# Attention times v on 64x32 array tiles instead of 64x64, in a talking-heads and Fourier-mix kernel

## The chip, the cores and the metric

One core of a Trainium2 chip. The metric is the device time of one execution in microseconds (us). The kernel before takes 2300.06 us, the median of three runs (2299.63 to 2300.28).

The engines are TensorE (PE, with its weight loader PEld), VectorE (DVE), ScalarE (ACT), GpSimd (POOL) and SyncE (SP, which only issues DMAs). PE multiplies a stationary operand, loaded by LDWEIGHTS, with a moving operand that streams through. Its array of 128 rows and 128 columns can be cut into tiles that work side by side: a "64x32" matmul uses 64 rows (the contraction) and 32 columns (the output partitions), so eight of them fill the array; of "64x64" ones four do. The names in the profile, such as `64*64`, are rows times columns of the matmul.

## The reference, cut to what matters

All data is float32. Eight batches, 12 heads, 448 positions, head dimension 64.

```python
scores = scale * np.matmul(q, k.transpose(0, 1, 3, 2))
scores = np.einsum('bhij,hg->bgij', scores, w_pre)       # heads mixed
attn = softmax(scores)
attn = np.einsum('bhij,hg->bgij', attn, w_post)          # heads mixed again
x = np.matmul(attn, v)                                   # the changed product
# then, with x as (8, 448, 768):
mixed = real(fft over channels of fft over positions of x)
u = x + mixed
un = layer_norm(u)
out = u + relu(un @ w_ch1) @ w_ch2                       # 768 -> 3072 -> 768
```

## The kernel before, in words

The program has two phases. The first does the attention and the Fourier mix (`mix_phase`), up to some 800 us; the second (`ffn_phase`) does the normalisation and the two large products, and isn't touched by the change. The weights are split and combined on DVE and POOL beside both phases.

**Steps.** The first phase runs 184 steps, 23 for each batch. A step handles some rows of the scores for all 12 heads. Its parts on PE are: the premix (`emit_premix`, L656; tile `mx`), the postmix of an earlier step (`emit_postmix`, L690; tile `po`), and the scores of a later block (`emit_qk`, L628; PSUM tiles `ms`). These three are issued as matmuls of 64 or 60 rows by 32 columns. DVE takes the maximum of `mx` (L663), ACT the exponential into `PP` (L670), DVE the reciprocal of the sums (L678), POOL the scaling (L680), and after the postmix DVE transposes `po` in blocks of 32 into the tile `Pv` (L703).

**Attention times v.** Once six or so steps have filled `Pv` (a group of two blocks), `emit_av` is called three times, each for two heads in each half of the head range (a pair `pr`): 8 batches x 4 groups x 3 pairs = 96 visits. A visit has seven key blocks (`jb`), which accumulate in PSUM. The two halves of the partitions (`y`) hold different heads and write to two PSUM tiles, `pss[0]` and `pss[1]`; the two heads of a half (`x`) write to output partitions 0 to 63 and 64 to 127. So it is 7 x 2 x 2 = 28 matmuls of 64 rows by 64 columns. The moving operand is a strided view of `Pv`: runs of five floats, 24 or 20 of them 224 floats apart, which makes 120 or 100 columns. The stationary operand is a 64x64 block of `v`. ACT then copies both PSUM tiles into `XT` (L489, the helper that all such copies share).

In the trace each of these float32 matmuls shows as two passes, each with its own weight load: 56 passes for a visit, 16 for a premix, a postmix or a score part.

**Other users of PE in this phase.** Transposes (L601, L764) and the two Fourier stages (L829, L845) have tile shapes of their own, with up to 128 rows and columns.

**Order.** On PE, DVE, ACT and POOL the order of the instructions is that of the program (a manual schedule). Two lists (`ORDERS`) say what each even and odd step does in which order; tables of steps (`AT_AV`, `AT_QK` and so on) say in which step each visit, score part, transpose and Fourier stage falls. The PSUM tiles `ms` come from a pool of four; every visit takes two.

Of the kernel before, what the change touches and what calls it, by code (L numbers as in the profile page):

```python
# [16 lines left out]
P = 128  # L17
B, NH, S, D = 8, 12, 448, 64
# [11 lines left out]
R = 5  # L30
# [119 lines left out]
def _ap(t: bass.AP, offset: int, dims) -> bass.AP:  # L150
    return bass.AP(tensor=t.tensor, offset=t.offset + offset,
                   ap=[list(d) for d in dims])
# [6 lines left out]
def _row(t: bass.AP) -> int:  # L159
    return t.ap[0][0]  # L160
# [290 lines left out]
def mix_phase(ctx, tc, rest, ident, q, k, v, w_pre, w_post, u_scr, u_rev, wts, lead):  # L451
# [36 lines left out]
    def copy(eng, out, in_):  # L488
        (nc.scalar.copy if eng == "a" else nc.vector.tensor_copy)(out=out, in_=in_)  # L489
# [11 lines left out]
    def ms_tile():  # L501
        return ms[-1]()
# [205 lines left out]
    def emit_av(a, pr):  # L708

        b, k = divmod(a, NG)  # L710
        st = batches[b]
        Pv = turned[a]["Pv"]
        rp = _row(Pv)
        nu = (GROUP_AT[k + 1] - GROUP_AT[k]) * 4
        pss = [ms_tile() for _ in range(2)]
        for jb in range(C7):
            for x in range(2):
                for y in range(2):
                    i = 2 * pr + x
                    nc.tensor.matmul(  # L720
                        pss[y][64 * x:64 * x + 64, :nu * R],
                        st["v", pr][64 * y:64 * y + 64, x, jb * D:(jb + 1) * D],
                        _ap(Pv, 64 * y * rp + 32 * jb + R * i,
                            [[rp, 64], [HS, nu], [1, R]]),
                        start=(jb == 0), stop=(jb == C7 - 1))
        g = groups[b * NG + BLOCKS[2 * k][3]]
        if pr == 0:
            g["XT"] = pxt.tile([P, 6, XW], F32, name="XT", tag="XT")
        XT = g["XT"]
        rx = _row(XT)  # L730

        def done(y):
            rs = _row(pss[y])
            c = 0
            for _, w, n, _, first, sg in BLOCKS[2 * k:2 * k + 2]:
                dst = _ap(XT, (3 * y + pr) * XW + PG[g["gi"]] + first,
                          [[rx, P], [sg * w, R], [sg, w]])
                src = _ap(pss[y], c, [[rs, P], [1, R], [R, w]])
                copy(ENG["AV"][y], dst, src)
                c += R * w  # L740
            if y == 1 and pr == 2:
                if k in SPILL:
                    gi, c0, n, go, co = SPILL[k]
                    Xo = groups[b * NG + go]["XT"]
                    back = -1 if gi == 2 else 1
                    nc.scalar.copy(
                        out=_ap(Xo, PG[go] + co, [[rx, P], [XW, 6], [1 - 2 * (go == 1), n]]),
                        in_=_ap(XT, PG[gi] + c0, [[rx, P], [XW, 6], [back, n]]))
                if k in NONE:
                    gi, cols = NONE[k]  # L750
                    for o in cols:
                        Xo = groups[b * NG + gi]["XT"]
                        nc.vector.memset(Xo[:, :, PG[gi] + o:PG[gi] + o + 1], 0.0)
        return [lambda y=y: done(y) for y in range(2)]
# [136 lines left out]
    for b in range(B):  # L891
# [31 lines left out]
        for n in range(NG):  # L923
            for pr in range(3):
                due("AV", f + GROUP_AT[n + 1] + AT_AV[n][pr],
                    lambda a=b * NG + n, pr=pr: (emit_av(a, pr), None))
            at, gi = AT_X[n]
            if b == B - 1 and n > 1:
                at += 2
            due("full", f + at, lambda g=groups[b * NG + gi]: emit_x(g))  # L930
# [623 lines left out]
```

## Time and profile before

| | |
|---|---|
| Median of three runs | 2300.06 us |
| Span of the profiled execution | 2297.6 us, 60793 instructions |
| The profiled execution's own time | the page gives its span alone; the median is 2.5 us above it |
| Granted TensorE clock | 0.998 |
| PE, PEld busy | 2249.2 us (98%), 1740.7 us (76%) |
| DVE, ACT, POOL busy | 1711.2 us (74%), 1167.1 us (51%), 1292.1 us (56%) |
| L720 on PE | 160.8 us busy, 5376 passes, 62.9 to 797.0 us |

How to read it: a row of a timeline is start, duration, engine, line, operation, output <- input, tile (rows*columns), shape, and count; in brackets stands the engine's idle time before it and what ended it ("issue": nothing that the profile shows). A row of a group is count | busy us, mean ns of one | idle time before, by what ended it. A row of waits is who waited for whom: us in total, times, the longest. In a row of the windows the numbers after the window are its length and then the busy time and count of each engine named in the head of the view. The ends of matmuls are modelled, their starts are recorded. Busy times of a line on PE count time in which several of its passes run as one.

### The profile page before, as it was taken

What the parts mean: (1) busy time and instruction counts of PE and PEld (TensorE: products, weight loads), DVE (VectorE), ACT (ScalarE), POOL (GpSimd) and SP (SyncE); (2) the same over time, 40 slices, a digit from 0 to 9 for tenths busy, and PEclk for the clock granted to TensorE, in tenths of its full rate; (3) what the DMA queues carried; (4) which work ended last, traced back from release to release, by engine and by line L of the source; (5) the groups of instructions that cost most, each with busy time, mean ns of one, the idle gap of its engine ahead of it and who ended that gap; (6) DMA issues with size and microseconds to landing.
All of it is one profiled execution on the core that took longest, in us unless ns stands there. A gap on an engine that the chain in (4) does not pass through costs nothing.

```text
span 2297.6 us, 60793 instructions
## 1 busy us (share of the span) xinstructions
PE 2249.2 (98%) x22894; PEld 1740.7 (76%) x22894; DVE 1711.2 (74%) x3640; ACT 1167.1 (51%) x3330; POOL 1292.1 (56%) x1805
## 2 busy tenths in 40 slices
PE   7999999999999999999999999999999999999998
PEld 3455555555554677777899999999999899999998
DVE  5778787888877757776877787778778777765545
ACT  4676767767676533231445445444444445434434
POOL 7677878879768541221555555546555645454334
PEclk9999999999999999999999999999999999999999
DMA  7566565666756475649677887788787987795664
GB/s 185 168 178 181 168 192 171 190 179 181 202 151 190 143 265 182 230 162 327 191 181 180 252 214 184 212 195 242 204 197 184 277 188 174 191 257 121 143 146 76
DMA packets 228063, 439.45 MB, mean 191 GB/s; under 512 B 35964, under 2 KB 149558, under 8 KB 227772
## 3 DMA queue, kind: packets, MB, share of 16 engines
q1 hardware_dynamic: 156620, 301.52, 38.2%
q0 software_dynamic: 68864, 133.00, 30.4%
q8 instruction: 183, 3.00, 0.6%
q10 hardware_dynamic: 2288, 1.05, 0.2%
q14 instruction: 108, 0.88, 0.1%
HBM read 213.16 MB, written 143.16 MB: 155 GB/s over the span
## 4 chain that ended last, share of the span: by engine, by line
PE 87%; DVE 5%; DMA 3%; ACT 2%; issue 1%; POOL 1%; SPq 1%; ACTq 0%; DVEq 0%; POOLq 0%
PE psP L1213 18%; PE psP L1335 14%; PE psR L1213 9%; PE psR L1335 7%; PE mx L656 6%; PE ms L720 6%; PE ms L628 5%; PE po L690 5%; PE psQ L1213 4%; PE psQ L1335 3%; PE psP L1290 3%; PE ms L845 2%; PE ms L601 2%; DMA Kr<-Sb 1%; PE psR L1290 1%
## 5 line engine op out<-in xcount | busy, mean ns | idle before, releaser
L1369 POOL DMA_DIRECT2D out_dram<-od x172 | 209.1, 1276 | 261.7 <-DVE od L1357 175.3
L680 POOL TENSOR_SCALAR PP<-PP,rcp 128x448 f32<-128x448 f32 x368 | 234.6, 647 | 170.2 <-DVE rcp L678 123.8
L670 ACT ACTIVATE PP<-mx,nmx 128x448 f32<-128x448 f32 x368 | 230.2, 631 | 165.2 <-DVE nmx L663 157.2
L663 DVE TENSOR_REDUCE nmx<-mx 128x1 f32<-128x448 f32 x368 | 212.5, 618 | 101.2 <-PE mx L656 99.1
L1176 POOL TENSOR_TENSOR hq<-h 128x128 f32<-128x128 f32 (+1 forms) x210 | 130.0, 619 | 255.9 <-ACT h L1235 122.3
L1363 ACT COPY od<-psP 128x192 f32<-128x192 f32 x488 | 156.1, 320 | 172.0 <-PE psP L1335 170.6
L1366 DVE TENSOR_TENSOR od<-od 128x768 f32<-128x768 f32 x210 | 201.3, 972 | 52.7 <-ACT od L1363 52.3
L703 DVE STREAM_TRANSPOSE Pv<-po 128x896 f32<-128x896 f32 x184 | 203.7, 1107 | 2.9 <-PE po L690 2.1
L489 ACT COPY Sb<-ms 124x448 f32<-124x448 f32 (+1 forms) x378 | 181.7, 540 | 46.0 <-PE ms L628 19.2
L656 PE MATMUL mx<-Kr,kw 60*32 60x448 f32 x2944 | 192.2, 549 | 4.3 <-ACT PP L670 2.3
L628 PE MATMUL ms<-kT,qT 64*32 64x448 f32 (+1 forms) x3072 | 191.6, 545 | 3.9 <-ACT qT L489 2.8
L720 PEld LDWEIGHTS ms<-Pv,vv 64*64 64x64 f32 x5376 | 138.1, 132 | 73.7 <-issue 48.8
L690 PE MATMUL po<-PP,kw 60*32 60x448 f32 x2944 | 184.0, 537 | 1.2 <-POOL PP L680 1.1
L1213 PE MATMUL psP<-qs,w1t 128*128 128x256 f32 x744 | 179.2, 380 | 2.4 <-DVE h L1234 1.5
L1213 PE MATMUL psP<-ks,w1t 128*128 128x256 f32 x744 | 179.3, 380 | 0.4 <-DVE h L1234 0.3
L720 PE MATMUL ms<-Pv,vv 64*64 64x120 f32 (+1 forms) x5376 | 160.8, 263 | 3.6 <-ACT Sb L489 2.2
L254 POOL TENSOR_SCALAR wst<-wst 128x256 f32<-128x256 f32 (+1 forms) x76 | 118.6, 1569 | 67.2 <-ACT wst L265 66.9
L1213 PEld LDWEIGHTS psP<-qs,w1t 128*128 128x128 f32 x744 | 139.5, 190 | 19.4 <-DVE h L1234 1.9
L1213 PEld LDWEIGHTS psP<-ks,w1t 128*128 128x128 f32 x744 | 139.5, 190 | 17.2 <-DVE h L1234 0.7
L1213 PE MATMUL psP<-ub,w1t 128*128 128x256 f32 x528 | 127.2, 379 | 1.1 <-DVE h L1234 1.1
L1234 DVE TENSOR_TENSOR h<-h,psP 128x512 f32<-128x512 f32 x42 | 28.8, 686 | 127.9 <-PE psP L1213 112.3
L1335 PE MATMUL psP<-w2t,hq 128*128 128x192 f32 x490 | 122.5, 332 | 1.2 <-DVE od L1357 1.2
(199 smaller groups left out, 5301.6 us busy)
## 6 DMA issues: line engine op xcount, KB each, us to landing
Kr<-Sb SPq DMA_DIRECT2D x730, 105.0 KB
out_dram<-od POOLq DMA_DIRECT2D x172, 384.0 KB, 6.3
qs<-ub SPq DMA_DIRECT2D x89, 384.0 KB
ks<-ub SPq DMA_DIRECT2D x88, 384.0 KB
ub<-ub SPq DMA_DIRECT2D x79, 384.0 KB
w1t<-w SPq DMA_DIRECT2D x42, 384.0 KB
w2t<-w SPq DMA_DIRECT2D x42, 384.0 KB
raw<-in_moe_w_ch_dram SPq DMA_DIRECT2D x32, 384.0 KB
```

The costliest lines, as they stand in the source:

```text
L628: nc.tensor.matmul(pss[x][o:o + hi - lo, :S], st["qT", xx][64 * x:64 * x + 64, y, lo:hi], st["kT", xx][64 * x:64 * x + 64, y, :], start=Tr ...
L656: nc.tensor.matmul(mx[x][64 * z + o:64 * z + o + 32, :S], kw1[64 * x:64 * x + KR, o:o + 32], Kr[64 * x:64 * x + KR, z, :], start=True, sto ...
L663: nc.vector.tensor_reduce(nmx[:, :], steps[T]["mx"][x][:, :S], axis=AX.X, op=ALU.max, negate=True)
L670: nc.scalar.activation(steps[T]["PP"][:, x, :], steps[T]["mx"][x][:, :S], ACTF.Exp, bias=steps[T]["nmx", x][:, :], accum_out=steps[T]["den ...
L680: nc.gpsimd.tensor_scalar(PP[:, x, :], PP[:, x, :], rcp[:, x:x + 1], 1.0, op0=ALU.mult, op1=ALU.mult)
L690: nc.tensor.matmul(po[o:o + 32, z, :S], kw2[64 * z:64 * z + KR, y, :], PP[64 * z:64 * z + KR, :, c * HS:(c + 1) * HS], start=True, stop=True)
L703: nc.vector.transpose(turned[a]["Pv"][:, j, :].rearrange("p (z s) -> p z s", z=2), steps[T]["po"][:, :, :S])
L720: nc.tensor.matmul(pss[y][64 * x:64 * x + 64, :nu * R], st["v", pr][64 * y:64 * y + 64, x, jb * D:(jb + 1) * D], _ap(Pv, 64 * y * rp + 32 ...
L1213: mm = nc.tensor.matmul(p[:, m, :], w1[i][:, kc, m * P:(m + 1) * P], ub[:, kc, :], start=i in (0, 4, 1)[:3 - seed] and m == kc == 0, stop= ...
L1335: nc.tensor.matmul(ps[j, key][:, :DQ], a, b, start=m in (0, 4), stop=True, skip_group_check=True)
L1366: eng.tensor_tensor(D[j][:, :, :], D[j][:, :, :], D[k][:, :, :], op=ALU.add)
L1369: nc.gpsimd.dma_start(out=acc[t, r, d], in_=D[j][:, :, :], accum_op=ALU.add)
```

## The change

Each matmul of attention times v is issued as two of half the width. The loop over the two heads `x` becomes a loop over the four offsets `o` = 0, 32, 64, 96 of the output partitions; `divmod(o, 64)` gives the head and the half of its 64 columns of v. The moving operand of both halves is the same view of `Pv` as before. The output lands in the same PSUM tiles at the same place, with the same accumulation over `jb`.

```diff
         for jb in range(C7):
-            for x in range(2):
+            for o in range(0, P, 32):
+                x, d = divmod(o, D)
                 for y in range(2):
                     i = 2 * pr + x
                     nc.tensor.matmul(
-                        pss[y][64 * x:64 * x + 64, :nu * R],
-                        st["v", pr][64 * y:64 * y + 64, x, jb * D:(jb + 1) * D],
+                        pss[y][o:o + 32, :nu * R],
+                        st["v", pr][64 * y:64 * y + 64, x, jb * D + d:jb * D + d + 32],
                         _ap(Pv, 64 * y * rp + 32 * jb + R * i,
                             [[rp, 64], [HS, nu], [1, R]]),
                         start=(jb == 0), stop=(jb == C7 - 1))
```

A visit now has 56 matmuls in place of 28, so 112 passes. The order of the program on PE in the middle of the phase, a visit between a postmix and a score part (`po` is the postmix, `ms<-kT,qT` the scores, `mx` the premix), before:

```order
L656 MATMUL mx<-Kr,kw_172 32x448 x8
L690 MATMUL po<-PP,kw_173 32x448 x8
L720 MATMUL ms<-Pv,vv 64x120 x28
L628 MATMUL ms<-kT,qT 32x448 x6
L628 MATMUL ms<-kT,qT 28x448 x2
L656 MATMUL mx<-Kr,kw_172 32x448 x8
```

and with the change:

```order
L656 MATMUL mx<-Kr,kw_172 32x448 x8
L690 MATMUL po<-PP,kw_173 32x448 x8
L721 MATMUL ms<-Pv,vv 32x120 x56
L628 MATMUL ms<-kT,qT 32x448 x6
L628 MATMUL ms<-kT,qT 28x448 x2
L656 MATMUL mx<-Kr,kw_172 32x448 x8
```

The visit keeps its place; its matmuls have 32 output columns in place of 64 and are twice as many (the first number of a shape is that of the output partitions). A few steps on, a visit of 100 moving columns between a score part and a premix, before:

```order
L690 MATMUL po<-PP,kw_173 32x448 x8
L628 MATMUL ms<-kT,qT 32x448 x6
L628 MATMUL ms<-kT,qT 28x448 x2
L720 MATMUL ms<-Pv,vv 64x100 x28
L656 MATMUL mx<-Kr,kw_172 32x448 x8
```

and with the change:

```order
L690 MATMUL po<-PP,kw_173 32x448 x8
L628 MATMUL ms<-kT,qT 32x448 x6
L628 MATMUL ms<-kT,qT 28x448 x2
L721 MATMUL ms<-Pv,vv 32x100 x56
L656 MATMUL mx<-Kr,kw_172 32x448 x8
```

Nothing around it moves, here or on the other engines; lines behind it in the file are one higher.

## The prediction, made before the changed kernel was run

> **What bounds the kernel now.** I read the page first: the shares of the engines, then the chain that ended last.
>
> ```profile
> PE 2249.2 (98%) x22894; PEld 1740.7 (76%) x22894; DVE 1711.2 (74%) x3640; ACT 1167.1 (51%) x3330; POOL 1292.1 (56%) x1805
> PE 87%; DVE 5%; DMA 3%; ACT 2%; issue 1%; POOL 1%; SPq 1%; ACTq 0%; DVEq 0%; POOLq 0%
> PE psP L1213 18%; PE psP L1335 14%; PE psR L1213 9%; PE psR L1335 7%; PE mx L656 6%; PE ms L720 6%; PE ms L628 5%; PE po L690 5%; PE psQ L1213 4%; PE psQ L1335 3%; PE psP L1290 3%; PE ms L845 2%; PE ms L601 2%; DMA Kr<-Sb 1%; PE psR L1290 1%
> ```
>
> TensorE (PE) carries 87% of the chain, and the changed line, L720, is 6% of the span on it. L720 runs only in the attention phase, so next comes the view of busy time by stage, for that phase:
>
> ```profile
> core 0: us, PE busy (x) PEld busy (x) DVE busy (x) ACT busy (x) POOL busy (x), PEclk, DMA share, GB/s
> 62.00:800.00 738.00, 720.47 (x14741) 392.83 (x14730) 591.87 (x1238) 507.98 (x1591) 570.46 (x886) 1.00 0.59 176
> ```
>
> There PE is busy for 720 of 738 us, VectorE (DVE) for 592, GpSimd (POOL) for 570. So PE sets the pace, but DVE at 80% has not much in hand. A busy PE here may hide time in which the array waits, since the ends of matmuls are modelled; so I go by starts. The timeline of PE, two ordinary steps:
>
> ```profile
> 400.91 0.96 PE L628 MATMUL ms<-kT,qT 64*32 64x448 f32 x16
> 401.80 1.70 PE L720 MATMUL ms<-Pv,vv 64*64 64x120 f32 x56
> 403.43 0.98 PE L656 MATMUL mx<-Kr,kw 60*32 60x448 f32 x16
> 404.21 0.96 PE L690 MATMUL po<-PP,kw 60*32 60x448 f32 x16
> 404.96 0.96 PE L628 MATMUL ms<-kT,qT 64*32 64x448 f32 x16
> 405.85 1.56 PE L845 MATMUL ms<-tcs,z 96*112 96x193 f32 x8
> ...
> 458.93 1.46 PE L720 MATMUL ms<-Pv,vv 64*64 64x100 f32 x56
> 460.32 0.98 PE L656 MATMUL mx<-Kr,kw 60*32 60x448 f32 x16
> ```
>
> Each matmul of the program shows as two passes (28 in the program's order are x56 here). From L690 to L628, both 64x32 tiles, it is 404.96 - 404.21 = 0.75 us for two passes on eight tiles: 0.837 ns per moving column. From L628 to L720, the same two passes, it is 0.89. The same 0.89 stands before L845, which has a third tile shape. So a change of shape costs 0.14 us at the entry.
>
> **The change part by part.** *The pass itself.* L720 takes 1.63 us to the next group with 120 columns and 460.32 - 458.93 = 1.39 with 100. Fourteen passes per tile lie in each, so 20 columns are 0.24/14 = 17 ns, 0.86 ns per column, the rate of the 64x32 groups. A pass of 120 columns is then 0.103 us and 14 of them 1.44; the remaining 1.63 - 1.44 = 0.19 us is not streaming. Afterwards eight tiles stream at once where four did, each half as wide: still seven products of two passes per tile, 14 x 0.103. So the streaming is worth nothing either way, as long as eight tiles keep up.
>
> *The two changes of shape.* The weight loader (PEld) shows where the 0.19 comes from:
>
> ```profile
> 401.80 1.47 PEld L720 LDWEIGHTS ms<-Pv,vv 64*64 64x64 f32 x56 [0.74 <-issue]
> 404.96 0.15 PEld L628 LDWEIGHTS ms<-kT,qT 64*32 64x32 f32 x8 [0.23 <-issue]
> ```
>
> Between groups of one shape the loads run ahead under the last pass (the loader idles 0.23 us). Before L720 it idles 0.74 and the loads begin only with the group, so the first ones lie open. Price of a visit: 0.14 at entry, 0.19 inside it and at its exit, and 403.43 to 404.21 = 0.78 instead of 0.75 for the premix that follows, 0.03: together 0.36 us. I take 0.35. All of it goes if L720 has the shape of its neighbours.
>
> *How many.* 5376 passes by 56 are 96 visits. By the order of the program 90 stand between two 64x32 groups and three more have one on one side; the last ones, in the tail, have none. 90 x 0.35 + 3 x 0.19 = 32 us of PE time.
>
> *What is added.* Loads and matmuls double, 56 to 112 each per visit.
>
> ```profile
> L720 PEld LDWEIGHTS ms<-Pv,vv 64*64 64x64 f32 x5376 | 138.1, 132 | 73.7 <-issue 48.8 <-ACT Sb L489 6.8 <-ACT X L489 5.6
> PEld ms L720 <- issue: 48.8, 68, 0.7
> L628 PEld LDWEIGHTS ms<-kT,qT 64*32 64x32 f32 x2304 | 54.6, 107 | 76.0 <-issue 53.7 <-ACT Sb L489 7.0 <-ACT qT L489 6.2
> ...
> 780.53:780.60 0.07, 0.06 (x8) 0.07 (x13) 1.00 0.66 263
> 458.93:460.17 1.24, 1.24 (x56) 1.24 (x56) 1.00 0.80 238
> ```
>
> A 32-column load takes 107 ns against 132, and it overlaps the pass before on its tile, as now. Whether PE can start so many is the open price. It needs eight matmuls and eight loads per 103 ns. From below: in the 0.07 us window of L690, right after the loader had stood idle, eight passes start and thirteen loads run, so eight starts take under 70 ns and hide under the 103. From above: the densest sustained run is the visit with 100 columns, 56 passes in 1.24 us, 22 ns each; were that a limit, eight would take 177 ns. I go with the burst, as it is the same tile shape and the 22 ns are explained by the columns (100 and 120 differ as the columns do). I allow 2 ns per pass for contention: 90 x 14 x 2 ns = 2.5 us back.
>
> The Trainium skill ("TensorE: Matmul & The Clock Gate", section "Wait — 56ns, not 53.3ns?") speaks against the change: starts of matmuls are never closer than about 25 ns however short they are. By that, as an estimate, a visit would take 112 x 25 ns = 2.8 us and the kernel lose some 97 us; the trace disagrees, with 22 ns over a whole visit and eight starts in 70 ns.
>
> The longer instruction stream is fetched in the shadow (packets, MB, share of the DMA engines):
>
> ```profile
> q8 instruction: 183, 3.00, 0.6%
> ```
>
> PE has 45,788 instructions and gets 10,752 more; a quarter more on a queue at 0.6% is nothing. PSUM tiles, evacuations, DMAs and the order on the other engines stay as they are. No wait is added; the visit's two waits for a free PSUM tile now stand ahead of its first load at the same place, with the same work queued behind them.
>
> *What is late next.* The 32 us count only where PE is the last to arrive. Premix needs the softmax's `mx` tile free, postmix needs the POOL scaling:
>
> ```profile
> PEld mx L656 <- ACT PP L670: 12.4, 34, 1.6
> PEld po L690 <- POOL PP L680: 12.1, 33, 1.2
> ...
> L656 PE MATMUL mx<-Kr,kw 60*32 60x448 f32 x2944 | 192.2, 549 | 4.3 <-ACT PP L670 2.3
> ...
> 405.80 0.62 ACT L670 ACTIVATE PP<-mx,nmx 128x448 f32<-128x448 f32 x1
> 407.34 0.98 PE L656 MATMUL mx<-Kr,kw 60*32 60x448 f32 x16
> ...
> 494.66 0.56 DVE L856 TENSOR_TENSOR X<-X,ms 112x385 f32<-112x385 f32 x1 [0.54 <-PE ms L845]
> 496.06 0.55 DVE L858 TENSOR_TENSOR X<-X,ms 112x383 f32<-112x383 f32 x1
> 496.22 1.70 PE L720 MATMUL ms<-Pv,vv 64*64 64x120 f32 x56
> 496.53 1.15 DVE L663 TENSOR_REDUCE nmx<-mx 128x1 f32<-128x448 f32 x2
> 497.87 0.62 ACT L670 ACTIVATE PP<-mx,nmx 128x448 f32<-128x448 f32 x1
> 498.63 0.96 PE L656 MATMUL mx<-Kr,kw 60*32 60x448 f32 x16
> ```
>
> In the ordinary step the second exp ends at 406.42 and premix follows 0.92 us later: a visit 0.35 shorter still finds it done. In the step at 496 the exp ends at 498.49, 0.14 before premix, because four additions of the Fourier stage (the first and the last are shown) stand ahead of the maxima (L663) on DVE; the visit's gain there turns into waiting. Ends by exp are 34 of the 2944/16 = 184 premixes, 18%: I take 18% of 90 visits as lost, 16 x 0.35 = 5.7 us. The 33 waits on POOL come in clusters where POOL falls behind for a few steps and catches up; most are short (0.37 us mean, where 0.22 is the loader's usual idle time). I put them at half as much again, 3 us.
>
> **The sum.** 32 - 2.5 - 5.7 - 3 = 20.8 us. The profiled span is 2297.6 us; the median of the runs is 2300.06, so 2.5 us lie around the span and are not touched. Span 2276.8, time 2300.06 - 20.8 = 2279.3, a shade over 0.9% faster. About 0.2% (4.6 us) is what a measurement here can tell from no change.
>
> **The rivals.**
>
> *All of it arrives.* The dependencies follow, because the exps and POOL are themselves started by PE: 2300 - 32 - a little = 2267. For it: the slack of 0.9 us in ordinary steps. Against: the two kinds of wait above exist already. 8%.
>
> *The gain is mostly swallowed.* DVE at 80% and POOL at 77% of the phase become the pace in more steps than counted, and PE waits for exp or scaling. A third or less of 32 us stays: 2290 to 2298. For it: the waits shown, and 21 us less phase would raise DVE only to 592/717 = 83%, which is against. 14%, of which 3% within 0.2%.
>
> *The stall isn't the shape's.* If L720 were late for another reason (its wait on Pv or on a PSUM tile), it stays: 2300. Against: the delay is 0.14 before L845 as well, and 0.74 of loader idle time repeats where no semaphore is named (48.8 us over 68 times, in the row of waits above). 4%.
>
> *PE can't start them (slower).* The place is each visit; the mechanism a limit on sustained starts at the 22 ns of the densest run. Then 112 x 22 ns = 2.46 us replace 1.44, 1.02 more, less the 0.35 saved: 0.67 x 96 = 64 us, 2364. It decides from 0.128 us per eight starts, 16 ns each, where 14 x 25 ns eat the 0.35. For it: no run in this trace sustains more than one start per 22 ns over a microsecond. Against: the burst. 7%.
>
> *Four tiles read the same rows of Pv (slower).* Two tiles share each half of the partitions now, four will, in runs of five floats. L628 reads with four already at the full rate, but contiguously. If each pass took 140 ns: 14 x 37 - 350 = +0.17 us a visit, 16 us, 2316; up to 128 ns per pass it costs no more than the gain. 4%, of which 1% within 0.2%. The Trainium skill ("SBUF — State Buffer", "Door 1: The DMA port swizzle") says that each crossing into a new 16-byte line pays a penalty; runs of 20 bytes cross often. The present 103 ns, 3 above 120 x 0.837, bound what two readers pay, and no run here shows four.
>
> **How the numbers follow.** The forecast itself has 63%, with its own range 2268 to 2290 (the losses at nothing or doubled). Faster by over 0.2%: 63 + 8 + 11 = 82%. Within 0.2%: 3 + 4 + 1 = 8%. Slower: 7 + 3 = 10%. The range of 8 in 10 reaches from the full gain, 2265, into the swallowed one, 2294, and leaves out the slow cases and the unchanged one.
>
> **What would show it.** Right: between two neighbours of 64x32 the visit of 120 columns goes from 1.63 to about 1.45 us and the group before it from 0.89 to 0.75; the loader's idle time before the line falls from 0.72 us per visit to about 0.22; x10752 passes, with the same 0.86 ns per column. More waits `PEld mx <- ACT PP` and `PEld po <- POOL PP`, by some 9 us. The rest of the program unchanged, only 21 us earlier. Wrong: visits longer than 1.63 us, with starts evenly spaced at 16 ns or more whether 100 or 120 columns (the start limit), or a pass that lengthens while bursts stay short (the reads), or an entry still 0.14 late (not the shape).

## The result, and the profile after

The changed kernel takes 2368.7 us (median of 4 runs, 2364.7 to 2370.3) against 2299.9 us before (4 runs, 2297.9 to 2300.3). The ratio is 1.029, with a 95% interval of 1.028 to 1.031: 3% slower, where 0.9% faster was forecast. The profiled execution of after has a span of 2367.1 us at a granted clock of 0.994.

First the page of after: the shares of the engines, the chain that ended last by engine, the instruction queue, and the two groups of the changed line.

```profile
PE 2271.2 (96%) x28270; PEld 1839.3 (78%) x28270; DVE 1705.8 (72%) x3640; ACT 1171.0 (49%) x3330; POOL 1291.8 (55%) x1805
...
q8 instruction: 225, 3.69, 0.7%
...
PE 89%; DVE 3%; issue 3%; ACT 2%; DMA 1%; POOL 1%; SPq 0%; DVEq 0%; ACTq 0%; POOLq 0%
...
L721 PEld LDWEIGHTS ms<-Pv,vv 64*32 64x32 f32 x10752 | 176.7, 105 | 88.3 <-issue 78.0
L721 PE MATMUL ms<-Pv,vv 64*32 64x120 f32 (+1 forms) x10752 | 196.2, 267 | 48.5 <-issue 47.6
```

Two things are new. "Issue", time in which an engine waits for nothing that the profile shows, is 3% of the chain where it was 1%. And TensorE itself, not only its weight loader, stands 47.6 us ahead of L721 with that label. The view of waits for the attention phase of after (us in total, times, longest us) gives their size:

```profile
ACT XT L489 <- PE ms L721: 82.9, 67, 6.8
PEld ms L721 <- issue: 78.0, 151, 3.5
PE ms L721 <- issue: 47.6, 40, 3.3
```

Before, the loader's idle time ahead of the line was 48.8 us in 68 pieces of at most 0.7; now it reaches 3.5, and ScalarE waits up to 6.8 us for a visit to end (3.7 before). The first matmul of the FFN shows that the loss lies ahead of it. The timeline of TensorE (start, duration), of before and then of after:

```profile
797.32 2.00 PE L1213 MATMUL psP<-qs,w1t 128*128 128x256 f32 x8
```

```profile
868.01 2.86 PE L1214 MATMUL psP<-qs,w1t 128*128 128x256 f32 x12
```

It starts 70.7 us later; from there to the end of the span it is 1500.3 us before and 1499.1 after. All of the loss is in the attention phase.

Inside that phase the timeline of after shows two kinds of visit. Two undisturbed groups first:

```profile
208.18 0.96 PE L628 MATMUL ms<-kT,qT 64*32 64x448 f32 x16
208.94 1.84 PE L721 MATMUL ms<-Pv,vv 64*32 64x120 f32 x110
210.51 0.57 PE L656 MATMUL mx<-Kr,kw 60*32 60x448 f32 x2
```

From L628 to L721 it is 0.76 us, no longer 0.89: the forecast change of shape at the entry is gone. The visit lasts 1.57 to the start of the next group, a little less than the 1.63 before, though not the 1.45 forecast. Then a visit that is cut (the last column is idle time before the row and its releaser):

```profile
174.09 1.11 PE L690 MATMUL po<-PP,kw 60*32 60x448 f32 x16
174.84 1.21 PE L721 MATMUL ms<-Pv,vv 64*32 64x100 f32 x69
179.34 1.07 PE L721 MATMUL ms<-Pv,vv 64*32 64x100 f32 x38 [3.28 <-issue]
```

and the loader's row in the same place:

```profile
179.34 0.86 PEld L721 LDWEIGHTS ms<-Pv,vv 64*32 64x32 f32 x40 [3.49 <-issue]
```

After 69 recorded passes TensorE stands still for 3.28 us, and its loader for 3.49. No semaphore, no DMA of data and no other engine is named.

**Reading the stalls.** The instruction queue moves packets of 3.69 MB / 225 = 16.4 KB. TensorE's records (loads, matmuls and its other instructions) are 57,788 after and 47,036 before; divided by the packets of 225 and 183 that is 257 in both. So a packet is a block of 256 of TensorE's instructions. I counted TensorE's records in order of start and noted every gap over 0.3 us at a border between two blocks at which a packet had landed 1.1 to 1.9 us earlier. In the attention phase there are 5 such gaps before, 3.0 us in all, and 69 after, 83.5 us. 67 of the 69 lie at one and the same record of a block, number 193 modulo 256. A few short ones may be chance, since starts 0.3 to 0.5 us apart occur between ordinary groups too; four of the five before are of that length.

This gives the **theory of instruction supply**: the next block's packet is fetched only when the block before has been begun, and takes some 4 us until its first instruction runs. A block that TensorE uses up faster is followed by a stall. A visit used to be 112 instructions (56 loads, 56 matmuls) of a block; it is 224 now, nearly a whole block, gone in 1.5 us. The rivals were that the shape or its reads of Pv cost the time, that each added instruction costs the same wherever it stands, and that starts are limited (the prediction's rival with 2364 us).

### The profile page after: what moved, and what is told of

Read it like the earlier page. It is cut to its first block, busy times and chain, and to the rows that moved or that the text cites. A ratio compares the mean times of both kernels' runs of the same rounds, so it can differ in the third digit from the quotient of the medians.

```text
span 2367.1 us, 71545 instructions
## 1 busy us (share of the span) xinstructions
PE 2271.2 (96%) x28270; PEld 1839.3 (78%) x28270; DVE 1705.8 (72%) x3640; ACT 1171.0 (49%) x3330; POOL 1291.8 (55%) x1805
## 3 DMA queue, kind: packets, MB, share of 16 engines
q8 instruction: 225, 3.69, 0.7%
## 4 chain that ended last, share of the span: by engine, by line
PE 89%; DVE 3%; issue 3%; ACT 2%; DMA 1%; POOL 1%; SPq 0%; DVEq 0%; ACTq 0%; POOLq 0%
PE psP L1214 17%; PE psP L1336 13%; PE psR L1214 9%; PE mx L656 7%; PE ms L721 7%; PE psR L1336 7%; PE ms L628 6%; PE po L690 5%; PE psQ L1214 4%; PE psQ L1336 3%; PE psP L1291 3%; PE ms L846 2%; PE ms L601 2%; PE psR L1291 1%; PE ms L830 1%
## 5 line engine op out<-in xcount | busy, mean ns | idle before, releaser
L721 PEld LDWEIGHTS ms<-Pv,vv 64*32 64x32 f32 x10752 | 176.7, 105 | 88.3 <-issue 78.0
L721 PE MATMUL ms<-Pv,vv 64*32 64x120 f32 (+1 forms) x10752 | 196.2, 267 | 48.5 <-issue 47.6
L628 PE MATMUL ms<-kT,qT 64*32 64x448 f32 (+1 forms) x3072 | 224.6, 546 | 7.2 <-issue 3.9
L656 PE MATMUL mx<-Kr,kw 60*32 60x448 f32 x2944 | 217.8, 554 | 9.0 <-DMA Kr<-Sb 4.8
L690 PE MATMUL po<-PP,kw 60*32 60x448 f32 x2944 | 212.3, 543 | 3.9 <-issue 3.9
L690 PEld LDWEIGHTS po<-PP,kw 60*32 60x32 f32 x2944 | 84.4, 107 | 66.6 <-issue 45.3
L628 PEld LDWEIGHTS ms<-kT,qT 64*32 64x32 f32 (+1 forms) x3072 | 85.2, 106 | 63.5 <-issue 37.0
```

The costliest lines, as they stand in the source:

```text
L628: nc.tensor.matmul(pss[x][o:o + hi - lo, :S], st["qT", xx][64 * x:64 * x + 64, y, lo:hi], st["kT", xx][64 * x:64 * x + 64, y, :], start=Tr ...
L656: nc.tensor.matmul(mx[x][64 * z + o:64 * z + o + 32, :S], kw1[64 * x:64 * x + KR, o:o + 32], Kr[64 * x:64 * x + KR, z, :], start=True, sto ...
L690: nc.tensor.matmul(po[o:o + 32, z, :S], kw2[64 * z:64 * z + KR, y, :], PP[64 * z:64 * z + KR, :, c * HS:(c + 1) * HS], start=True, stop=True)
L721: nc.tensor.matmul(pss[y][o:o + 32, :nu * R], st["v", pr][64 * y:64 * y + 64, x, jb * D + d:jb * D + d + 32], _ap(Pv, 64 * y * rp + 32 * j ...
```

## The experiments

**The same number of instructions without the shape.** The tiles stay 64x64, but each matmul is cut in two along its moving columns (60 or 50 in place of 120 or 100), which also gives 224 instructions a visit.

```diff
-            for x in range(2):
-                for y in range(2):
+            for c in range(0, nu, nu // 2):
+                for x in range(2):
+                    for y in range(2):
...
-                        pss[y][64 * x:64 * x + 64, :nu * R],
+                            pss[y][64 * x:64 * x + 64, c * R:(c + nu // 2) * R],
...
-                            [[rp, 64], [HS, nu], [1, R]]),
+                                [[rp, 64], [HS, nu // 2], [1, R]]),
...
```

> The kernel before, its 64x64 tiles kept, with each matmul of attention times v cut in two along the moving columns (60 or 50 each) instead of along the heads' columns. It has exactly as many TensorE instructions as the changed kernel (224 a visit in place of 112), the same streaming, and both changes of tile shape remain. Theory of instruction supply (TensorE's instructions arrive in blocks of 256, the next block about 4 us after the one before was begun; a visit of 224 in 1.5 us outruns it): stalls ended by 'issue' inside and behind the visits, at every 256th instruction or so, some 70 to 90 of them, and 2360 to 2415 us. Theory of the tile shape (64x32 tiles are slow here, by four readers of the same rows or a limit on starts of eight tiles): 2300 to 2315 us, the upper end because passes of 50 to 60 columns hardly cover a load of 64.

Measured: 2370.9 us against 2295.1 there, ratio 1.033 (1.031 to 1.034). The waits of this kernel and one undisturbed visit from its timeline:

```profile
PEld ms L721 <- issue: 86.3, 100, 3.9
```

```profile
214.89 1.86 PE L721 MATMUL ms<-Pv,vv 64*64 64x60 f32 x112
216.68 0.98 PE L656 MATMUL mx<-Kr,kw 60*32 60x448 f32 x16
```

The old shape with the new count of instructions loses as much as the change, 75.8 us; 2370.9 lies within the 2360 to 2415 us that the theory of instruction supply expected. By the count of gaps it has 63 stalls, 59.5 us (70 to 90 stalls were expected). The visits themselves are longer too, 1.79 us where 1.63 stood, and by the starts of the undisturbed ones 1.78 where 1.39 stood with 100 columns in two halves of 50; over 96 visits that is an estimated 20 us. First to last start is 1.64 us at 60 columns and 1.63 at 50, so the columns don't set it any more. Whether the count of instructions does (224 at 7.3 ns) or the twice as many loads of 64 columns was not separated. That the shape or the reads alone are to blame is refuted.

**The shape at few instructions.** Here a visit takes four of the seven blocks of keys, and reads runs of ten floats in place of five, so 240 or 200 moving columns (part of the computation is left out, and the rest isn't what the reference sums). One kernel does this with 64x64 tiles, 64 instructions a visit, the other with 64x32 tiles, 128 a visit.

```diff
-        for jb in range(C7):
+        for jb in range(4):
...
-                        pss[y][64 * x:64 * x + 64, :nu * R],
+                        pss[y][64 * x:64 * x + 64, :2 * nu * R],
...
-                            [[rp, 64], [HS, nu], [1, R]]),
+                            [[rp, 64], [HS, nu], [1, 2 * R]]),
...
```

> The kernel before with four of the seven key blocks in attention times v, and runs of ten floats in place of five as moving columns (240 or 200 columns, half of them not used; the outputs are no longer the reference's). A visit streams 4 x 2 x 0.2 = 1.6 us instead of 1.44, but has 64 TensorE instructions in place of 112. Partner of the next run. Both theories: the visits get some 0.16 us longer, 2300 to 2316 us, no stalls by issue.

> The changed kernel (64x32 tiles) with the same four key blocks and runs of ten floats: 128 TensorE instructions a visit, about what the kernel before has, in 1.6 us. Instruction supply: hardly any stalls, and the changes of tile shape are saved, so 15 to 27 us under the 64x64 partner, near 2285 to 2295. Tile shape: not faster than the partner, 2305 us or more.

Measured: 2309.7 us (ratio to before 1.0058, 1.0042 to 1.0075) with 64x64, 2301.0 us (1.0022, 1.0010 to 1.0034) with 64x32. The first lies in its expected range; the smaller tiles are 8.7 us faster, less than the 15 to 27 expected. The timelines, 64x64 first:

```profile
201.91 0.96 PE L628 MATMUL ms<-kT,qT 64*32 64x448 f32 x16
202.80 1.85 PE L720 MATMUL ms<-Pv,vv 64*64 64x240 f32 x32
204.59 0.98 PE L656 MATMUL mx<-Kr,kw 60*32 60x448 f32 x16
```

```profile
407.12 0.96 PE L628 MATMUL ms<-kT,qT 64*32 64x448 f32 x16
407.87 1.83 PE L721 MATMUL ms<-Pv,vv 64*32 64x240 f32 x64
409.49 1.13 PE L656 MATMUL mx<-Kr,kw 60*32 60x448 f32 x16
```

Entry 0.89 and 0.75, visit 1.79 and 1.62: together 0.31 us saved per visit, nearly the 0.35 of the prediction. Of 96 x 0.31 = 30 us, 7.3 go into 8 stalls at borders (none with 64x64), 8.7 arrive, and the other 14 are lost on the way; the profile doesn't itemise them.

The 30 us are a rough estimate, because the rows above stand for two of the three pairs of heads. With 64x64 tiles 23 of the 24 visits of 240 columns for the middle pair (`pr` = 1) took 2.11 us: by the starts, two of the four tiles needed 0.245 us a pass where the others needed 0.203. With 64x32 tiles the same pair has slow tiles again (first to last start 1.78 us in the median), but the next group starts on the other tiles at 1.62. What makes these runs of Pv slow was not sought. The fast passes take 0.203 us with two readers of the same rows and with four, so at runs of ten floats four readers cost nothing that can be seen; runs of five, which the change has, this pair doesn't test.

**More instructions, spread.** The kernel before, with scores and premix cut in two along their columns: 12,032 instructions more, above the change's 10,752, but each group of 64 spread over its former time.

```diff
-        for y in range(2):
+        for h, y in ((h, y) for h in (0, HS) for y in range(2)):
...
-                        pss[x][o:o + hi - lo, :S],
+                        pss[x][o:o + hi - lo, h:h + HS],
...
```

> The kernel before with the scores and the premix cut in two along the moving columns (224 each): 12,032 TensorE instructions more, over a tenth more than the change adds, but spread over all steps; a premix or score part has 64 in 0.75 us, the visits stay as they were. Instruction supply by density (blocks that are used up in under some 4 us stall): fewer and shorter stalls than the change has, 2310 to 2345 us. If every added instruction cost the same as in the change (69 us / 10,752 = 6.4 ns): 2377. If the number of instructions doesn't matter: 2300.

Measured: 2322.7 us, ratio 1.0115 (1.0084 to 1.0146), with 31 stalls of 25.4 us together. More instructions than the change added cost +28 us in place of +69, inside the range expected from supply. A fixed price per instruction is refuted, and so is that spread instructions are free: in places the blocks get short enough here too.

**Where the border falls.** Only 14 of the 96 visits get 64x32 tiles, all others keep 64x64. The 14 were picked so that a visit lies nearly whole in one block. The second kernel has the same 14 and, at the very start of TensorE's program, 32 one-column matmuls (128 instructions, half a block), which move every border. The third has the 32 matmuls alone.

```diff
+        w = 32 if 3 * a + pr in [5, 7, 9, 16, 17, 33, 53, 59, 67, 69, 70, 77, 83, 89] else 64
...
+            for o in range(0, P, w):
+                x, d = divmod(o, D)
...
```

```diff
+    def ahead():
+        for _ in range(4):
+            ps = ms_tile()
+            for _ in range(8):
+                nc.tensor.matmul(ps[:32, :1], ident[:, :32], ident[:, :1], start=True, stop=True)
+
+    due("none", -42, ahead)
```

> 14 of the 96 visits (numbers 5, 7, 9, 16, 17, 33, 53, 59, 67, 69, 70, 77, 83, 89 in the program's order) use 64x32 tiles, the other 82 stay 64x64: 14 x 112 = 1568 instructions more for TensorE than in the kernel before. The 14 were picked by laying blocks of 256 instructions over TensorE's records of the kernel before so that nearly all of each visit's 224 instructions fall into one block. Instruction supply (a block of 256 that is used up in less than about 4 us is followed by a stall until the next one has come): each of the 14 is cut by a stall of 1 to 2.5 us, some 14 stalls, the kernel 17 to 32 us slower than before (1.007 to 1.014). Rival, every added instruction or every 64x32 visit costs the same: the +69 us of the full change over 96 visits is 0.72 us a visit, so +10 us (1.0044).

> The same 14 visits, with 32 one-column matmuls (128 instructions of TensorE) added at the very start of its program, while it waits for the first loads: all block borders move by half a block, and each of the 14 visits now lies across a border, half of its instructions on each side. Instruction supply: no stall, or one or two, in those visits; -2 to +2 us against before (0.999 to 1.001). Rival, a cost per instruction or per visit: as without the shift, +10 us (1.0044), both kernels alike.

> The kernel before with the 32 one-column matmuls at the start alone, the control of the shift. Both theories: -1.5 to +1.5 us (0.9993 to 1.0007), since TensorE waits for the first loads there and a block with visits of 112 instructions lasts over 4 us wherever its borders fall.

Measured, against 2297.2 us of before there:

| kernel | us | ratio, 95% interval | stalls at borders |
|---|---|---|---|
| 14 visits | 2305.2 | 1.0040 (1.0025 to 1.0056) | 16, 13.5 us |
| 14 visits, shifted | 2298.8 | 1.0008 (0.9998 to 1.0018) | 12, 8.7 us |
| before, shifted | 2297.7 | 1.0000 (0.9987 to 1.0013) | 8, 6.5 us |

One of the 14 visits in the timelines, without the shift and with it:

```profile
175.73 0.96 PE L628 MATMUL ms<-kT,qT 64*32 64x448 f32 x16
176.48 1.64 PE L722 MATMUL ms<-Pv,vv 64*32 64x100 f32 x106
179.93 0.36 PE L722 MATMUL ms<-Pv,vv 64*32 64x100 f32 x5 [1.81 <-issue]
```

```profile
177.97 0.96 PE L628 MATMUL ms<-kT,qT 64*32 64x448 f32 x16
178.72 1.80 PE L722 MATMUL ms<-Pv,vv 64*32 64x100 f32 x111
180.29 0.57 PE L656 MATMUL mx<-Kr,kw 60*32 60x448 f32 x3
```

The same instructions on the same data stall for 1.81 us or not at all, by where the border lies. The unshifted kernel's +8 us alone would have fitted the fixed price as well (+10); the shifted one doesn't, its interval ends at 1.0018. Without the shift TensorE went on after each border behind one of the 14 visits 1.0 to 1.5 us after the packet had landed, the mark of a late packet; with it the borders inside 13 of the 14 visits show gaps of at most 65 ns (the other one 1.34 us), and both shifted kernels came out as expected. The expected size, 17 to 32 us, was too large: the stalls were 0.1 to 2.1 us each, about 10 us together, and some blocks with such a visit went by in 2.7 to 2.9 us where the block before had lasted 5 to 7. A fixed 4.1 us from block to block, which lay behind that expectation, is too simple. The 6.4 us between the first two kernels are a difference of medians. In their profiled executions the FFN began at 803.5 and 803.4 us, and the profiled one of the shifted kernel took 2303.4 us, the longest of its 12; so the medians and the gaps inside the visits carry this argument, not the totals of the profiles.

**The price by itself.** 7168 instructions at the start of the kernel before, on eight 64x32 tiles, in blocks whose streaming takes longer and longer.

```diff
+        for n, blocks in ((4, 8), (240, 8), (320, 8), (448, 4)):
+            pss = [ms_tile() for _ in range(2)]
+            for _ in range(8 * blocks):
+                for o in range(0, P, 32):
+                    for y in range(2):
+                        nc.tensor.matmul(pss[y][o:o + 32, :n], ident[64 * y:64 * y + 64, :32],
+                                         _ap(ident, 64 * y * ri, [[ri, 64], [1, 4], [0, n // 4]]),
+                                         start=True, stop=True)
```

> The kernel before with 7168 instructions for TensorE added at the very start: matmuls on eight 64x32 tiles, in four stretches of 8, 8, 8 and 4 blocks of 256 instructions (64 matmuls each), with 4, 240, 320 and 448 moving columns. By the rate of 0.837 ns per column the array needs almost nothing, 3.2, 4.3 and 6.0 us for a block. This measures the disputed cost by itself; the end of the kernel only shifts. Instruction supply: a block of 256 can't follow the one before in less than about 4.1 us (3.4 to 6.4), so the blocks of 4 columns take some 4 us each, in bursts with stalls between them, those of 240 columns about 4 us too, with a short stall each, those of 320 and 448 columns what the array needs, 4.3 and 6.0 us, without stalls. Rival, a limit on starts (the 7 ns per instruction of the visits in halves): 256 x 7 ns = 1.8 us for a block of 4 columns, evenly spaced, and 3.2, 4.3 and 6.0 us for the others, no stalls.

Measured: 2413.1 us against 2303.3 there, one run each; the blocks themselves are what counts. The timeline of the weight loader; each row is the 128 loads of one block. Three blocks of 4 columns, then three of 240:

```profile
26.16 1.28 PEld L955 LDWEIGHTS ms<-ident 64*32 64x32 f32 x128 [2.45 <-issue]
29.89 1.28 PEld L955 LDWEIGHTS ms<-ident 64*32 64x32 f32 x128 [2.45 <-issue]
33.62 1.28 PEld L955 LDWEIGHTS ms<-ident 64*32 64x32 f32 x128 [2.45 <-issue]
...
52.80 3.17 PEld L955 LDWEIGHTS ms<-ident 64*32 64x32 f32 x128 [0.57 <-issue]
56.52 3.17 PEld L955 LDWEIGHTS ms<-ident 64*32 64x32 f32 x128 [0.56 <-issue]
59.98 3.17 PEld L955 LDWEIGHTS ms<-ident 64*32 64x32 f32 x128 [0.28 <-issue]
```

and the DMA view of the same kernel from 26 to 37 us, when nothing else moved data, in 40 slices of 0.275 us:

```profile
DMA  0000200000000000003000000000000200000000
...
q8 instruction: 3, 0.05, 1.9%
```

A block of 4 columns runs for 1.3 us and is followed by a stall of 2.45: 3.73 us from block to block. The first packet shows in slice 5, about 1.1 us after the first instruction of the block before; by its record it takes 1.1 us, and its own instructions follow 1.5 us after that. One fetch at a time, begun about when the block before has been begun. (In the attention phase of the changed kernel the packet begins between 0.6 us before and 5.6 us after the first instruction of the block before, in the median 1.4 after; no first instruction comes less than 1.2 us after its packet has landed.) At 240 columns the array needs 3.2 us and the stall shrinks to 0.3 to 0.6, 3.5 to 3.7 us from block to block. At 320 columns it goes; the windows from 70 to 88 us:

```profile
core 0: us, PE busy (x), PEclk, DMA share, GB/s
70.00:88.00 18.00, 18.00 (x544) 1.00 0.01 4
```

The array is busy throughout. The 544 count some 13 passes that lie only partly inside; by the starts a block of 128 passes takes 4.34 us, the 4.3 of the columns, and there is no gap at the borders. Earlier, while the kernel's first loads ran, two blocks of 4 columns took 6.8 and 6.2 us. The limit on starts (1.8 us for a block, evenly) is refuted as the cause of the loss: a block's starts lie within 1.16 us, and the stall behind them is twice as long.

The Trainium skill ("Runtime: NRT & Kernel Launch", section "Instruction fetch mechanics") describes blocks of 16 KiB or 256 instructions, of which the next is fetched while the current one runs, and calls the cost of crossing to a new block mostly hidden. The size and the fetch of one block ahead agree with these runs; that it is hidden holds here for the blocks of 4.34 us (DMA queues quiet), and not for the 1.3 to 3.2 us of the blocks above.

## Why the prediction was wrong

**The step that failed** is in the part on what is added: "The longer instruction stream is fetched in the shadow ... a quarter more on a queue at 0.6% is nothing." The share of a queue says how much bandwidth is used, not how late a packet comes. The row after it is 0.7%, as small as forecast, and the stalls went from 3.0 to 83.5 us. What counts is how soon TensorE uses up a block: a visit of 112 instructions in 1.63 us left time for the next packet, one of 224 in 1.57 mostly doesn't. Shown by the old shape with the new count (+76 us), by the shift of the border, and by the block of 3.73 us.

**The entry**, 0.14 us a visit: right. 0.89 became 0.76 in the rows above.

**The visit at 1.45 us**: wrong, 1.57. Of the 0.19 us inside the visit and at its exit 0.17 did go where columns set the pace (1.79 to 1.62 us at 240 columns). With 120 columns it was 0.07 in the median: a pass took 112 ns in place of the 103 + 2 forecast, so the term "2 ns per pass for contention" was mis-sized. The visits of 100 columns gained nothing inside: the median of the 8 undisturbed ones is 1.41 us to the next group, 1.39 before. What stretches them is open. It is no fixed time per instruction: 224 instructions take 7.0 ns each with 120 columns and 6.3 with 100, and in the blocks of 4 columns 256 start within 1.16 us, 4.5 ns each. Reads of the same rows by four tiles in runs of five floats were not tested by themselves.

**The sum, redone with what was measured.** If all visits went like the undisturbed ones, 72 visits of 120 columns would gain 0.14 + 0.07 and 24 of 100 columns about 0.14 - 0.02: an estimated 15 + 3 = 18 us in place of the 32 less 2.5. The stalls cost 83.5 - 3.0 = 80.5. That makes +62; the FFN began 70.7 us later. The other 8 us are not itemised; other engines' waits grew too (ScalarE for L721 from 21.5 to 82.9 us), but whether these make the 8 was not tested.

**The losses to exp and POOL**, 8.7 us: the changed kernel can't show them, because its phase is longer. In the pair at 240 columns 14 of some 30 us didn't arrive, stalls apart, so 8.7 may have been low; its cause there wasn't sought.

**The rivals.** "PE can't start them" gave 2364 us, near the measured 2368.7, at 7%. Its number was right by chance: it put 22 ns on every start, evenly; measured are 112 starts in 1.61 us (the visit at 208.94), 14 ns each, and stalls at borders. The burst of eight starts in 70 ns, which the prediction set against it, held: the blocks of 4 columns keep eight starts and eight loads per 73 ns up for 1.16 us. "Four tiles read the same rows" is refuted as the cause of the loss by the visits cut along columns, which keep two readers and lose as much; a share in the 112 ns it may have. "The stall isn't the shape's" is refuted by the entry; the other two were on the wrong side. Of the prediction's own signs of error, the entry spoke for it, the evenly spaced starts were not seen, and no sign was named for instructions that come late.

## What to carry to other kernels

Before splitting matmuls into more, smaller ones, count the instructions of the dense stretches. Here blocks of 256 of TensorE's instructions, one behind the other, had to last some 3.5 to 3.7 us each with quiet DMA queues and up to 7 with busy ones, or the array stood still until the next block had come. A single short block, of 2.4 to 3.0 us, sometimes passed without a stall, behind a block that had lasted long. A group of 224 instructions in 1.6 us is too dense where most of it falls into one block; 13 of 14 such groups that lay across a border passed. With fewer, longer passes (240 columns) the smaller tile was 8.7 us faster than the larger one.

In a profile this shows as "issue" on both PE and PEld, 0.3 to 3.5 us long and often in the middle of a group, at the same count modulo 256; the share of the instruction queue doesn't show it.

## What the runs showed of the hardware that was not expected

- With the DMA queues quiet, the packet of the next block of TensorE's instructions starts about 1.1 us after the block before has begun, takes 1.1 us, and 1.5 more pass until its first instruction: 3.73 us per block of 256, and 6.2 to 6.8 with the kernel's first loads running.
- Within a block 128 loads and 128 matmuls of 4 columns on eight tiles started within 1.16 us, 4.5 ns each. In the dense visits it was 6.3 to 7.3 ns; what sets these was not separated.
- Changing the tile shape between groups cost 0.14 us at the entry and 0.17 inside the group and at its exit, by the pair at 240 columns.
- With 64x64 tiles and moving operands in runs of ten floats, two of the four tiles took 0.245 us for a pass of 240 columns where the others took 0.203, in the visits of one pair of heads in three; the cause is open.
- Moving all borders by half a block changed the median of a kernel by 0.3% (2305.2 and 2298.8 us) with the same instructions behind it.

A version that beats the kernel before was not found: the 14 shifted visits, all but free of stalls at their own borders, stayed within 0.2% of it. Visits that take two groups at once, with 240 columns and half the instructions, were not tried; they would need a second buffer of Pv.
